# Reordering batch 1's q product and the last chunk of a fused attention and GLU kernel

## The chip, the cores and the metric

The kernel runs on one core of a Trainium2 chip. Its engines work beside each other and meet at semaphores: TensorE (PE in the profile, its weight loads PEld), VectorE (DVE), ScalarE (ACT), GpSimd (POOL) and SyncE (SP), which here only issues DMAs. The metric is the time of one execution on the device in microseconds. A run's time is a little longer than the span of its profile, which goes from the first instruction to the last.

## What is computed

```python
def phi(x):                                   # S1, S2: 8 x 32
    a = np.einsum('rd,bhsd->bhsr', S1, x)
    b = np.einsum('rd,bhsd->bhsr', S2, x)
    return np.einsum('bhsi,bhsj->bhsij', a, b).reshape(*x.shape[:-1], 64)
q_p, k_p = phi(q), phi(k)                     # q, k, v: batch 4, heads 4, sequence 1088, depth 32
kv = np.einsum('bhsf,bhsd->bhfd', k_p, v)
z = np.sum(k_p, axis=2)
num = np.einsum('bhsf,bhfd->bhsd', q_p, kv)
den = np.einsum('bhsf,bhf->bhs', q_p, z)[..., None] + 1e-06
x = (num / den).transpose(0, 2, 1, 3).reshape(4352, 128)
gate = 1.0 / (1.0 + np.exp(-(x @ w_gate)))    # w_gate, w_val: 128 x 1536
out = (gate * (x @ w_val)) @ w_out            # w_out: 1536 x 128
```

All data are fp32.

## The kernel before

**The second half sets the beat.** The 4352 tokens go in nine chunks: eight of 512 and a last one of 256. The 1536 hidden columns are 12 blocks of 128. A *wave* (`w1`, matmuls on L496) is one block of one chunk: gate and value products in one PSUM tile of two banks, from a pool of two such tiles. ACT takes the sigmoid of the gate half (`sg`, L504). DVE multiplies it with the value half (`g`, L537), which frees the tile for the wave after next. In the last chunk a wave covers two blocks of 256 tokens, so that it has six waves, and its gate is two DVE instructions (L530).

**The product with w_out follows some waves later.** A list `todo` holds each part with the wave number from which it may run. Chunk 0 uses plain products (`w2`, L379; two waves later). When the last of them is done, DVE transposes the result (L388) and SP issues four stores of 64 KB (L350). Chunks 1 to 7 take pairs of waves by a scheme with seven half products: `w2_a` (three waves after the odd wave) and `w2_b` (four), matmuls on L338. POOL makes the differences of tokens that they need (L328). At a chunk's end ACT copies part of the result and DVE adds (L435), spread over later waves by a list `late`. Chunk 8 uses `w2_end` (L400; three waves later, six parts of eight matmuls). Two half tiles of 128 tokens are collected in one PSUM tile of two banks, copied out by ACT (L409) and DVE (L410) into one SBUF tile, and stored by SP and ACT (L363). That SBUF tile and all earlier output tiles come from one tag, `o_sb`, with two buffers.

**`slot(group, waves)`** writes the order out by hand. It runs `group`, and then for each wave: the gate of the wave before (`glu`), one entry of `late` (two in the last chunk), all parts of `todo` that are due, and the next wave.

**The first half is fitted in between, batch by batch.** For batch 1 the steps are: transposes of k and q on DVE; `begin(1)`, which runs the gate, the k products (`kps`, L623) and the compact q products (`cqps`, L769), copies the latter to SBUF on ACT (L777), and then calls `spread`; the outer products for k (L702) and their sums (L876); the product of k with v (`kvz`, L842); two multiplies `qmult(1, 0)` and `qmult(1, 1)` on DVE (L822); and `parts(1)`, the numerators (L1207) and denominators (L971, L984).

**`spread`** turns the compact q products, 288 KB, into two operands of 1.1 MB: SP writes them to DRAM (`dq<-cq`, L787), waits until that has landed, and reads them back with repeats: `qp` and `bq` for the first q half, then for the second (L794), then eight small tables (L815). A `qmult` waits for the three reads of its half. The buffer of `bq` is the one that the next batch's k and q are loaded into.

PE, DVE, ACT and POOL run their instructions in the order of the program text. SP's DMAs are placed by the build, and each takes one of eight completion semaphores in turn, so that an issue can also wait for an older DMA on the same one.

Of the kernel before, what the change touches and what calls it, by code (L numbers as in the profile page):

```python
# [8 lines left out]
F32 = mybir.dt.float32  # L9
# [5 lines left out]
MUL = ALU.mult  # L15

P = 128
# [3 lines left out]
def kernel(  # L21
# [12 lines left out]
    nc = tc.nc  # L34

    B, H, S, D = q.shape
    R = S1.shape[0]
    F = R * R
    NTOK, DM = out.shape
    DFF = moe_w_gate.shape[1]  # L40
    NJ = DFF // P
    assert DM == H * D == P and D == 32 and R == 8 and S % 32 == 0 and NTOK % 512 == 256

    T = S // 32
# [4 lines left out]
    TCH = 512  # L49
# [292 lines left out]
    def store(ci, rows):  # L342
        t0, tw = tok_chk[ci]
        c = t0
        while c < t0 + tw:
            b, r = divmod(c, S)
            n = min(t0 + tw - c, S - r) // 32
            u = (c - t0) // 32
            for g4 in range(4):
                nc.sync.dma_start(  # L350
                    out=bass.AP(
                        tensor=out.tensor,
                        offset=out.offset + (b * S + r // 32) * DM + 32 * g4,
                        ap=[[T * DM, 32], [DM, n], [1, 32]],
                    ),
                    in_=rows(g4)[:, u : u + n, :],
                )
            c += n * 32

    def store_end(o_sb):  # L360
        b, r = divmod(tok_chk[-1][0], S)
        for c, eng in enumerate((nc.sync, nc.scalar)):
            eng.dma_start(  # L363
                out=bass.AP(
                    tensor=out.tensor,
                    offset=out.offset + (b * S + r // 32 + 16 * c * T) * DM,
                    ap=[[T * DM, 16], [1, 8 * DM]],
                ),
                in_=o_sb[64 * c : 64 * c + 64],
            )  # L370

    def w2(ci, j0, jn, g):
        if j0 == 0:
            moe["sum"] = ci
            moe["acc"] = pso.tile([P, TCH], F32, tag="acc0", name="moeout")
        for jj in range(jn):
            j = j0 + jj
            for d in (slice(0, P),) if j < NJ - 2 else (slice(0, 64), slice(64, P)):
                nc.tensor.matmul(  # L379
                    out=moe["acc"][d],  # L380
                    lhsT=w_sb[:, 2, j, d],
                    rhs=g[:, jj],
                    start=(j == 0),
                    stop=(j == NJ - 1),
                )
        if j0 + jn == NJ:
            o_sb = sbA.tile([P, 2, TCH // 32, 32], F32, tag="o_sb", name="o_sb")[:, 0]
            nc.vector.transpose(out=o_sb.rearrange("p t d -> p (t d)"), in_=moe["acc"])  # L388
            store(ci, lambda g4: o_sb[32 * g4 : 32 * g4 + 32])

    def w2_end(ci, j0, jn, g):
        if j0 == 0:
            moe["sum"] = ci
            moe["acc"] = ps2.tile([P, 2, TCH], F32, tag="two", name="moeout")
        acc = moe["acc"]
        for u in range(2):
            for jj in range(jn):
                j = j0 + jj
                for c in (u * P, u * P + 64):
                    nc.tensor.matmul(  # L400
                        out=acc[c % P : c % P + 64, u, :DM],
                        lhsT=g[:, jj, c : c + 64],
                        rhs=w_sb[:, 2, j, :],
                        start=(j == 0),
                        stop=(j == NJ - 1),
                    )
        if j0 + jn == NJ:
            o_sb = sbA.tile([P, 2, P], F32, tag="o_sb", name="o_end")
            nc.scalar.copy(out=o_sb[:, 0], in_=acc[:, 0, :DM])  # L409
            nc.vector.tensor_copy(out=o_sb[:, 1], in_=acc[:, 1, :DM])  # L410
            store_end(o_sb)


    fst = {}
# [66 lines left out]
    def w1():  # L481

        ci = moe["ci"]
        t0, tw = tok_chk[ci]
        jn = TCH // tw
        j0 = moe["w"] * jn
        wv = psm.tile([P, 2, TCH], F32, tag="wave", name="wave")

        tp = tw // 2 if ci == 0 and j0 == 0 else tw
        turn = (moe["w"] // 2) % 2  # L490
        for o in range(0, tw, tp):
            for which in range(2):
                for jj in range(jn):
                    for c in (0,) if ci == 0 else (1 - turn, turn):
                        d = slice(0, P) if ci == 0 else slice(64 * c, 64 * c + 64)
                        nc.tensor.matmul(  # L496
                            out=wv[d, which, jj * tw + o : jj * tw + o + tp],
                            lhsT=w_sb[:, which, j0 + jj, d],
                            rhs=xT[:, t0 + o : t0 + o + tp],
                            start=True,  # L500
                            stop=True,
                        )
        sg = sbG.tile([P, TCH], F32, tag="sg", name="sg")
        nc.scalar.activation(out=sg, in_=wv[:, 0], func=ACTF.Sigmoid)  # L504
        if ci == 0:
            if j0 == 1:
                narrow_01(2, 3)
            if 0 < j0 < NJ - 2:
                narrow_w(j0 + 1, 3)
            narrow_w(j0 + 2, 1)  # L510
            narrow_w(j0 + 2, 2)
            if j0 < 3:
                narrow_w(j0 + 3, 0)
            if j0 > 1:
                narrow_w(j0 + 4, 0)
            if j0 == NJ - 3:
                weight_sums(0, NJ // 4)
        if ci == 1 and j0 == 1:
            weight_sums(NJ // 4, NJ // 2)
        if moe["w"] % 2 == 0:  # L520
            moe["g"] = sbG.tile([P, 2, TCH], F32, tag="g", name="g")
        pair, odd, n = moe["g"], moe["w"] % 2, moe["n"]

        def glu():
            g = pair[:, odd]
            todo = moe["todo"]
            if jn == 2:
                for jj in range(2):
                    cols = slice(jj * tw, jj * tw + tw)
                    nc.vector.tensor_tensor(  # L530
                        out=g[:, cols].rearrange("p (u s y) -> p y u s", u=2, y=4),
                        in0=wv[:, 1, cols].rearrange("p (y u s) -> p y u s", u=2, y=4),
                        in1=sg[:, cols].rearrange("p (y u s) -> p y u s", u=2, y=4),
                        op=MUL,
                    )
            else:
                nc.vector.tensor_tensor(out=g, in0=wv[:, 1], in1=sg, op=MUL)  # L537
            if not fast(ci):
                lag = 3 if ci else 2
                part = (ci, j0, jn, g.rearrange("p (j t) -> p j t", j=jn))  # L540
                todo.append((n + lag, lambda: (w2_end if ci else w2)(*part)))
                return
            if not odd:
                moe["t"] = raw.tile([P, 4, HALF], F32, tag="w_in", name="tsum")
            token_sums(pair, moe["t"], odd)
            if odd:
                part = (ci, j0 // 2, pair, moe["t"])
                todo.append((n + 3, lambda: w2_a(*part)))
                todo.append((n + 4, lambda: w2_b(*part)))

        moe["gate"] = glu
        moe["w"] += 1
        moe["n"] += 1
        if j0 + jn == NJ:
            moe["ci"] += 1
            moe["w"] = 0
# [3 lines left out]
            moe["gate"]()  # L560
            moe["gate"] = None

    def slot(group, waves):

        if group is not None:
            group()
        todo = moe["todo"]
        for _ in range(waves):
            more = moe["ci"] < len(tok_chk)
            if more and sum(tok_chk[moe["ci"]]) > moe["ready"]:  # L570
                break
            glu()
            for _ in range(2 if moe["ci"] >= len(tok_chk) - 1 else 1):
                if moe["late"]:
                    moe["late"].pop(0)()
            while todo and todo[0][0] <= moe["n"]:
                todo.pop(0)[1]()
            if more:
                w1()
            elif not todo:  # L580
                break
            else:
                todo.pop(0)[1]()
# [236 lines left out]
    def qmult(b, n):  # L820
        q0 = half(QP[b], n)
        nc.vector.tensor_tensor(out=q0, in0=q0, in1=half(BQ[b], n), op=MUL)  # L822
# [358 lines left out]
    def begin(b):  # L1181
        glu()
        kps(b)
        cq[b] = qcomp(b, (0, 1), (psm, "wave"))
        spread(b, (0, 1), cq[b], nc.sync, nc.sync)
# [78 lines left out]
    slot(None, 1)  # L1264
    turn_q(1, 0)
    turn_q(1, 1)
    slot(lambda: begin(1), 1)
    for pi in range(2):
        outer(1, pi)
        slot(None, 1)  # L1270
# [7 lines left out]
    qmult(1, 0)  # L1278
    weights_z(1)
    slot(lambda: ndt(1), 1)  # L1280
    qmult(1, 1)
    load_kq(2)
    slot(None, 2)
    slot(lambda: parts(1), 1)

    def until(n):
# [63 lines left out]
```

## Time and profile before

| what | value |
|---|---|
| median of three runs | 296.4 us (295.51 to 296.53) |
| the profiled execution | 296.06 us |
| its span in the profile | 294.3 us |
| PE busy | 287.0 us, 98% of the span |
| chain that ended last: PE wave L496 | 51% |
| chain that ended last: PE prod L338 | 20% |
| chain that ended last: DMA qp<-dq | 4% |
| clock granted to PE | 1.00 |

In the profile a line reads: start, duration, engine, source line, operation, result and operands, count, and in brackets how long the engine stood idle before it and whose work ended that. In the chain of waits each piece is what the next one waited for, from the start to the last instruction. The ends of matmuls are modelled, so a short stall of PE can hide under the tail of the matmul before it; the distance from one wave's start to the next shows it better.

### The profile page before, as it was taken

The page shows a single profiled execution, that of the slowest core. Times are in us where ns is not written, and L with a number is a line of the kernel's source. Part 1 is how long each engine was busy: PE and PEld are TensorE (multiplying, and loading weights), DVE is VectorE, ACT ScalarE, POOL GpSimd, SP SyncE. Part 2 cuts the span into 40 slices and gives each one's busy share as a digit, 9 for nine tenths or more (in the row PEclk, how much of TensorE's full clock was granted, in tenths as well). Part 3 has the DMA queues.
Part 4 walks back from the last instruction along what each step waited for, and adds up shares of the span by engine and source line. Part 5 has one row for each costly group of instructions (what it writes and reads, how often), then busy time and mean ns, then how long its engine had stood idle before and what let it go on. Part 6 is the DMA issues. An engine that isn't in the chain of part 4 may idle for free.

```text
span 294.3 us, 5800 instructions
## 1 busy us (share of the span) xinstructions
PE 287.0 (98%) x2276; PEld 154.6 (53%) x2276; DVE 188.5 (64%) x326; ACT 92.1 (31%) x168; POOL 161.2 (55%) x221
## 2 busy tenths in 40 slices
PE   8899999999999999999999999999999999999994
PEld 3444433354455455554555555554555555555894
DVE  5998789977637766677556685668336433642463
ACT  3457542322223322322233213423232223322231
POOL 2365644894645657546446597664465655555200
PEclk9999999999999999999999999999999999999999
DMA  7993521584800167416000573102000200020002
GB/s 217 339 352 85 140 75 78 146 156 131 240 0 0 21 150 172 134 46 181 8 0 2 148 178 103 17 2 37 0 2 0 36 2 0 0 38 0 2 0 56
DMA packets 28762, 24.23 MB, mean 82 GB/s; under 512 B 18560, under 2 KB 23936, under 8 KB 28736
## 3 DMA queue, kind: packets, MB, share of 16 engines
q1 hardware_dynamic: 28288, 23.10, 30.2%
q10 hardware_dynamic: 448, 0.77, 0.9%
q8 instruction: 18, 0.29, 0.4%
q14 instruction: 8, 0.07, 0.1%
HBM read 20.60 MB, written 3.26 MB: 81 GB/s over the span
## 4 chain that ended last, share of the span: by engine, by line
PE 78%; DMA 7%; DVE 7%; POOL 2%; issue 2%; ACT 1%; SPq 1%; ACTq 0%; POOLq 0%
PE wave L496 51%; PE prod L338 20%; DMA qp<-dq 4%; POOL head L118 2%; PE moeout L400 2%; DVE head L109 2%; DMA kq<-in_k_dram 2%; DVE w_sb L127 2%; PE moeout L379 1%; DMA b<-dq 1%; DVE head L105 1%; PE nps L1207 1%; DVE qp L822 1%; PE kvz L842 1%; DMA dq<-cq 1%
## 5 line engine op out<-in xcount | busy, mean ns | idle before, releaser
L496 PE MATMUL wave<-xT,w_sb 128*64 128x512 f32 (+3 forms) x820 | 211.2, 566 | 0.6 <-DVE g L537 0.5
L496 PEld LDWEIGHTS wave<-xT,w_sb 128*64 128x64 f32 (+1 forms) x820 | 85.2, 140 | 64.4 <-issue 49.5
L504 ACT ACTIVATE sg<-wave 128x512 f32<-128x512 f32 x102 | 60.9, 597 | 173.8 <-PE wave L496 166.8
L537 DVE TENSOR_TENSOR g<-wave,sg 128x512 f32<-128x512 f32 x96 | 65.8, 686 | 75.3 <-ACT sg L504 74.1
L328 POOL TENSOR_TENSOR tsum<-g 128x256 f32<-128x256 f32 x84 | 67.8, 810 | 27.7 <-DVE g L537 27.5
L328 POOL TENSOR_TENSOR tsum<-g,tsum 128x256 f32<-128x256 f32 x42 | 34.2, 815 | 59.8 <-DVE g L537 59.6
L338 PE MATMUL prod<-tsum,ws 128*64 128x256 f32 x252 | 62.9, 381 | 0.0
L338 PEld LDWEIGHTS prod<-tsum,ws 128*64 128x64 f32 x252 | 31.3, 137 | 16.6 <-issue 12.3
L338 PE MATMUL prod<-g,w_sb 128*64 128x256 f32 x168 | 34.9, 383 | 0.0
L328 POOL TENSOR_TENSOR tsum<-tsum,g 128x256 f32<-128x256 f32 x42 | 32.7, 779 | 3.3
L338 PE MATMUL prod<-tsum,w_sb 128*64 128x256 f32 x84 | 25.4, 384 | 0.0
L338 PEld LDWEIGHTS prod<-g,w_sb 128*64 128x64 f32 x168 | 15.8, 137 | 18.2 <-issue 15.4
L338 PE MATMUL prod<-g,ws 128*64 128x256 f32 x84 | 25.0, 379 | 0.0
L118 POOL TENSOR_TENSOR head<-head,tail 128x384 int32<-128x384 int32 (+2 forms) x14 | 13.3, 953 | 18.2 <-DVE head L109 12.9
L338 PEld LDWEIGHTS prod<-g,ws 128*64 128x64 f32 x84 | 11.5, 137 | 3.8
L379 PE MATMUL moeout<-g,w_sb 128*128 128x512 f32 (+1 forms) x28 | 12.7, 611 | 0.3 <-DVE w_sb L127 0.3
L338 PEld LDWEIGHTS prod<-tsum,w_sb 128*64 128x64 f32 x84 | 10.9, 137 | 2.4 <-issue 1.9
L822 DVE TENSOR_TENSOR qp<-qp,bq 128x1152 f32<-128x1152 f32 (+1 forms) x7 | 9.6, 1376 | 3.4 <-DMA b<-dq 1.9
L702 DVE TENSOR_TENSOR kp<-kab 128x1152 f32<-128x1152 f32 (+2 forms) x10 | 10.8, 1094 | 0.0
L530 DVE TENSOR_TENSOR g<-wave,sg 128x256 f32<-128x256 f32 x12 | 6.6, 634 | 6.2 <-ACT sg L504 6.1
L470 DVE STREAM_TRANSPOSE o_sb<-res 64x512 f32<-64x512 f32 x14 | 9.5, 686 | 0.0
L435 DVE TENSOR_TENSOR res<-prod,other 64x512 f32<-64x512 f32 (+1 forms) x14 | 7.6, 541 | 2.6 <-ACT other L429 2.6
(121 smaller groups left out, 202.6 us busy)
## 6 DMA issues: line engine op xcount, KB each, us to landing
qp<-dq SPq DMA_DIRECT2D x7, 576.0 KB, 10.4
bq<-dq SPq DMA_DIRECT2D x14, 288.0 KB
kq<-in_k_dram SPq DMA_DIRECT2D x3, 544.0 KB, 4.0
kq<-in_q_dram SPq DMA_DIRECT2D x3, 544.0 KB
w_in<-in_moe_w_out_dram SPq DMA_DIRECT2D x6, 256.0 KB
w_in<-in_moe_w_gate_dram SPq DMA_DIRECT2D x5, 256.0 KB
w_in<-in_moe_w_val_dram SPq DMA_DIRECT2D x5, 256.0 KB, 6.9
out_dram<-o_sb SPq DMA_DIRECT2D x20, 64.0 KB, 1.9
```

Of the source, the lines that this page charges most:

```text
L118: nc.gpsimd.tensor_tensor(out=head, in0=head, in1=tail, op=ALU.add)
L328: nc.gpsimd.tensor_tensor(out=t[:, u], in0=in0, in1=in1, op=ALU.subtract)
L338: nc.tensor.matmul(out=out, lhsT=lhsT, rhs=rhs, start=start, stop=stop, skip_group_check=True)
L379: nc.tensor.matmul(out=moe["acc"][d], lhsT=w_sb[:, 2, j, d], rhs=g[:, jj], start=(j == 0), stop=(j == NJ - 1),)
L435: nc.vector.tensor_tensor(out=out, in0=in0, in1=in1, op=op)
L470: nc.vector.transpose(out=o_sb[:64, d].rearrange("p t x -> p (t x)"), in_=r[:, 1 + 2 * d : 3 + 2 * d].rearrange("p u x -> p (u x)"),)
L496: nc.tensor.matmul(out=wv[d, which, jj * tw + o : jj * tw + o + tp], lhsT=w_sb[:, which, j0 + jj, d], rhs=xT[:, t0 + o : t0 + o + tp], sta ...
L504: nc.scalar.activation(out=sg, in_=wv[:, 0], func=ACTF.Sigmoid)
L530: nc.vector.tensor_tensor(out=g[:, cols].rearrange("p (u s y) -> p y u s", u=2, y=4), in0=wv[:, 1, cols].rearrange("p (y u s) -> p y u s", ...
L537: nc.vector.tensor_tensor(out=g, in0=wv[:, 1], in1=sg, op=MUL)
L702: eng.tensor_tensor(out=KP[b][:, pi, j0:j1].rearrange("p j m (i l) -> p (j m) i l", i=R), in0=bass.AP(tensor=a0.tensor, offset=a0.offset, ...
L822: nc.vector.tensor_tensor(out=q0, in0=q0, in1=half(BQ[b], n), op=MUL)
```

## The change

Batch 1: `begin(1)` runs after the due w_out products of its slot instead of ahead of them, `qmult(1, 1)` and the load of batch 2's k and q come one slot later, and chunk 0's stores are put into `late`, to be issued with the next wave. In the built order of SP's queue, two of the four stores stand ahead of `dq<-cq` and two between it and the first `qp<-dq`; before, two stood between them and two after all of `spread`. The number of SP's DMAs is the same.

Last chunk: the gate is one DVE instruction per wave instead of two. The lag of `w2_end` is four waves instead of three. The last pair of chunk 7 (`early`) is multiplied one wave sooner. The two half tiles of the output lie in two PSUM tiles (tags `acc0` and `two`) and are copied into two SBUF tiles of tag `o_sb`, each stored by one engine as 128 runs of 512 B; before, each store had 64 runs of 1 KB.

```diff
-    def store_end(o_sb):
+    def store_end(acc):
         b, r = divmod(tok_chk[-1][0], S)
-        for c, eng in enumerate((nc.sync, nc.scalar)):
+        o_sb = [sbA.tile([P, P], F32, tag="o_sb", name="o_end") for _ in range(2)]
+        for u, copy in enumerate((nc.scalar.copy, nc.vector.tensor_copy)):
+            copy(out=o_sb[u], in_=acc[u])
+        for u, eng in enumerate((nc.scalar, nc.sync)):
             eng.dma_start(
                 out=bass.AP(
                     tensor=out.tensor,
-                    offset=out.offset + (b * S + r // 32 + 16 * c * T) * DM,
-                    ap=[[T * DM, 16], [1, 8 * DM]],
+                    offset=out.offset + (b * S + r // 32 + u) * DM,
+                    ap=[[T * DM, 32], [2 * DM, 4], [1, DM]],
                 ),
-                in_=o_sb[64 * c : 64 * c + 64],
+                in_=o_sb[u],
             )
...
-            store(ci, lambda g4: o_sb[32 * g4 : 32 * g4 + 32])
+            moe["late"].append(
+                lambda: store(ci, lambda g4: o_sb[32 * g4 : 32 * g4 + 32])
+            )
 
     def w2_end(ci, j0, jn, g):
         if j0 == 0:
             moe["sum"] = ci
-            moe["acc"] = ps2.tile([P, 2, TCH], F32, tag="two", name="moeout")
+            moe["acc"] = [
+                pso.tile([P, TCH], F32, tag="acc0", name="moeout0")[:, :DM],
+                ps2.tile([P, 2, TCH], F32, tag="two", name="moeout1")[:, 0, :DM],
+            ]
...
-                        out=acc[c % P : c % P + 64, u, :DM],
+                        out=acc[u][c % P : c % P + 64],
...
-            o_sb = sbA.tile([P, 2, P], F32, tag="o_sb", name="o_end")
-            nc.scalar.copy(out=o_sb[:, 0], in_=acc[:, 0, :DM])
-            nc.vector.tensor_copy(out=o_sb[:, 1], in_=acc[:, 1, :DM])
-            store_end(o_sb)
+            store_end(acc)
...
             if jn == 2:
-                for jj in range(2):
-                    cols = slice(jj * tw, jj * tw + tw)
-                    nc.vector.tensor_tensor(
-                        out=g[:, cols].rearrange("p (u s y) -> p y u s", u=2, y=4),
-                        in0=wv[:, 1, cols].rearrange("p (y u s) -> p y u s", u=2, y=4),
-                        in1=sg[:, cols].rearrange("p (y u s) -> p y u s", u=2, y=4),
-                        op=MUL,
-                    )
+                nc.vector.tensor_tensor(
+                    out=g.rearrange("p (j u s y) -> p j y u s", j=2, u=2, y=4),
+                    in0=wv[:, 1].rearrange("p (j y u s) -> p j y u s", j=2, u=2, y=4),
+                    in1=sg.rearrange("p (j y u s) -> p j y u s", j=2, u=2, y=4),
+                    op=MUL,
+                )
...
-                lag = 3 if ci else 2
+                lag = 4 if ci else 2
...
-                todo.append((n + 3, lambda: w2_a(*part)))
-                todo.append((n + 4, lambda: w2_b(*part)))
+                early = ci == len(tok_chk) - 2 and j0 == NJ - 1
+                todo.append((n + 3 - early, lambda: w2_a(*part)))
+                todo.append((n + 4 - early, lambda: w2_b(*part)))
...
-    def slot(group, waves):
+    def slot(group, waves, behind=None):
...
             while todo and todo[0][0] <= moe["n"]:
                 todo.pop(0)[1]()
+            if behind is not None:
+                behind()
+                behind = None
             if more:
                 w1()
...
-    slot(lambda: begin(1), 1)
+    slot(None, 1, behind=lambda: begin(1))
...
     slot(lambda: ndt(1), 1)
+    slot(None, 1)
     qmult(1, 1)
     load_kq(2)
-    slot(None, 2)
+    slot(None, 1)
     slot(lambda: parts(1), 1)
```

## The prediction

> **What bounds the kernel now.** I read the page first (shares, then the chain), then the chain in order of time, then the timelines of DVE, SP and the last 7 us, and the table of DMA issues.
>
> ```profile
> PE 287.0 (98%) x2276; PEld 154.6 (53%) x2276; DVE 188.5 (64%) x326; ACT 92.1 (31%) x168; POOL 161.2 (55%) x221
> ```
>
> TensorE (PE) is the bound, and almost without gaps: from 20 us to 290.4 us the window table shows 0.10 us idle in 40:60, 0.52 us in 60:80, and nothing else. No matmul is added or removed, so only three places can pay: the two stalls near 51 and 73 us, and what follows the last matmul. In order of time the chain of waits names the first two:
>
> ```profile
> 51.45 0.79 PE cqps L769 x16
> 52.26 0.65 ACT cq L777
> 52.93 2.08 DMA dq<-cq
> 56.94 10.88 DMA qp<-dq
> 67.84 4.01 DMA b<-dq
> 71.84 1.36 DVE qp L822
> 73.86 1.94 PE wave L496 x8
> ```
>
> Batch 1's q product is written to DRAM, read back spread, and multiplied on DVE. The second product (71.84) holds the gate of the wave that started at 67.95; the wave at 73.86 needs that gate's bank. DVE alone:
>
> ```profile
> 66.27 1.79 DVE L822 TENSOR_TENSOR qp<-qp,bq 128x1024 f32<-128x1024 f32 x1 [1.43 <-DMA bq<-dq]
> ...
> 69.23 0.68 DVE L537 TENSOR_TENSOR g<-wave,sg 128x512 f32<-128x512 f32 x1
> 71.84 1.36 DVE L822 TENSOR_TENSOR qp<-qp,bq 128x1152 f32<-128x1152 f32 x1 [1.93 <-DMA b<-dq]
> ```
>
> DVE idles twice for landings. The first wait costs PE nothing: the gate behind it ends at 69.91, and the wave that needs it starts at 70.54. The second does cost. SP's queue:
>
> ```profile
> 52.93 0.33 SPq L787 DMA_DIRECT2D dq<-cq  x1
> 53.97 0.87 SPq L350 DMA_DIRECT2D out_dram<-o_sb  x2
> 55.03 0.57 SPq L794 DMA_DIRECT2D qp<-dq  x1
> ```
>
> So the read-back starts when dq has landed, with two of chunk 0's stores issued in between; the other two come at 72.19. The end:
>
> ```profile
> 290.46 0.27 ACT L409 COPY o_end<-moeout 128x128 f32<-128x128 f32 x1 [2.11 <-PE moeout L400]
> 290.76 0.29 DVE L410 COPY o_end<-moeout 128x128 f32<-128x128 f32 x1 [1.27 <-ACT o_end L409]
> 291.08 0.62 ACTq L363 DMA_DIRECT2D out_dram<-o_end  x1
> 291.11 0.63 SPq L363 DMA_DIRECT2D out_dram<-o_end  x1
> ```
> ```profile
> out_dram<-o_sb SPq DMA_DIRECT2D x20, 64.0 KB, 1.9
> ...
> out_dram<-o_end SPq DMA_DIRECT2D x1, 64.0 KB, 2.3
> ```
>
> (The smallest stores, 16 KB, show 1.5 in the same column.) The two copies run one after the other, both stores start after the second, and they issue in 0.62 us side by side and land late (2.3 us).
>
> **What the Trainium skill says.** "Perfetto Trace Analysis", Per-instruction lifecycle (DMA Instruction, HWDGE): an issue locks the shared descriptor generator, and the recorded issue includes that lock wait. The trace agrees: two simultaneous issues took 0.62 and 0.63 us, a lone one (dq) 0.33. "DMA: Bandwidth & Descriptors", Queues, rings and completion order: on each DMA engine a queue's descriptors are taken up in ring order, so a store issued ahead on SP's queue is moved ahead. Before has no case of stores ahead of dq; I rest the delay below on it. The same page, Specifications: at least 512 B per transfer for full rate, below that slower. The new last stores have runs of exactly 512 B, the old ones 1 KB; no run here separates the two. "PSUM — Partial Sum Buffer", PSUM bank collisions: two engines must not use one bank and quadrant at once. The two halves of the old tile lie in different banks, so the 0.30 us between the copies is a dependency, not a bank.
>
> **The change part by part.** Times are on the clock of before.
>
> 1. *Chunk 0's last products ahead of batch 1's projections.* Removed: cqps starts at 51.45, 0.74 us after kps, though it takes 0.65 when nothing holds it (kps holds the same 16 records). Chunk 0's last product (0.91) then covers that wait, and the next wave's bank is free already (gate done at 52.15). New: product 50.61 to 51.5, kps 51.57, cqps 52.22, wave 52.87 instead of 53.01. Gain 0.14.
>
> 2. *The spread starts later.* cqps moves from 51.45 to 52.22; the copy ended 1.45 us after its start, so at 53.67; dq can be issued at 53.7. In the built order SP has two stores ahead of it. Their transpose (0.72) runs on DVE right after the gate, to 52.8; the stores issue 52.85 to 53.7 (0.87 for two). So SP is free just in time and dq is issued at 53.72, +0.79. The stores' data are partly ahead of dq's in the rings: 0 to 0.3 us more, I take 0.1. Stores three and four go out behind dq while it lands (2.08), so they cost the read-back nothing. All landings shift by s = 0.9; bounds 0.7 (nothing in the rings) and 1.5 (both stores' data fully ahead, and a lane wait).
>
> 3. *What s does.* The first multiply waits on a landing, so it and the gate behind it shift by s: gate ends at 69.91 + 0.9 = 70.81, wave at 70.86. PE would now be ready at 70.54 − 0.14 = 70.40. New stall 0.46, where there was none: gate slack 0.44 against s 0.9.
>
> 4. *The second multiply a slot later.* The gate that stood behind it now stands before it. The old stall: the wave at 70.54 takes 1.77 and the products after it 0.81, as in the pairs beside it, so 73.12 was possible and 73.86 came: 0.74 (0.52 shown; the rest is the modelled tail of the last matmul). It goes. The multiply now runs 72.74 to 74.1, the next gate to 74.8; the numerators want both at about 75.5. Covered by 0.7; beyond s = 1.6 it would cost. The next batch's k and q loads wait for this multiply, but were issued at 75.23 behind v's four, so they lose nothing.
>    Sum of 1 to 4: the wave at 73.86 moves to 70.86 + 2.58 = 73.44, gain 0.42. In general the gain is 1.32 − s, at most 0.88. PE is packed from there on, so it reaches the end.
>
> 5. *The last chunk.* Six gates, each two instructions taking 1.10, become one instruction each. Below: 0.69, as for a plain 512; above: 1.10. Nothing waits in either case, see 6.
>
> 6. *Lag four and one pair of products earlier.* On PE the same instructions in another order. Last sequence before: three parts after the last wave, 48 records in 2.79, at 0.87 per 16 a 2.61: stall 0.17 on the last gate. After, four parts (3.48) follow the last wave; sigmoid and gate need about 1.9, so the stall goes. New risks: the third and fourth waves stand back to back, the fourth needs the second's gate, with 0.6 us spare by my count; the sixth needs the fourth's gate, behind 2.03 us of chunk 7's sums on DVE: 0.4 spare. The early products need token differences that POOL finished at 273.88; they start at 274.66. Gain 0.17.
>
> 7. *Two PSUM tiles.* Tile 0's products end 0.43 before tile 1's, so ACT's copy is done before PE ends and its store leaves early. DVE copies straight after the last matmul: 0.30 gained. The DVE copy now waits for chunk 7's stores, because the second end tile takes their buffer. They leave two gates earlier (about 285.2 instead of 287.71); even if the last again lands 4.7 us after the first issue (the fourth was issued from 290.5 and takes 1.9) that is 289.9, before PE's end at 290.24. Covered, by 0.3.
>
> 8. *The last store's landing.* Old: 2.3 after issue, beside ACT's and right behind chunk 7's fourth store (issued until 291.01). New: alone, 64 KB in 128 runs. Bounds: 2.3 (nothing changes) and 1.5 (the smallest stores of the trace land so); I take 1.7. Gain 0.6.
>
> Sum: 0.42 + 0.17 + 0.30 + 0.60 = 1.5 at full value; I take off 0.1 for the doubled number of descriptors in the last stores, so 1.4. The profiled execution took 296.06 (span 294.3 and 1.76 around it): 294.7. Against the median of 296.4 it is 295.0. The three runs scatter over 1.0; I say 294.8.
>
> **The rivals.**
> A, the forecast: 294.8.
> B, the transfer takes the stall's place: s near 1.4, so the middle gives −0.1, and the last store still lands after 2.3: the end gives 0.47. 296.06 − 0.4 = 295.7. For it: each store's data are many small packets, and nothing in before shows dq behind them; against: dq is issued when most of them have gone.
> C, both stalls go: s at or under 0.44, the middle gives 0.88; the end gives 1.1: 294.1. For it: DVE waits 1.43 for the first landing, so any faster read-back is worth its full length; against: cqps alone starts 0.77 later.
> D, slower: dq is held by the stores, at SP's queue near 53 us, since the first store waits for DVE's transpose and everything behind it on SP waits too. Price 1:1 from s = 1.32; with 1.07 from the end it is slower from s = 2.4, and by over 0.5% from 3.9. At s = 4: 296.06 + 2.7 − 1.07 = 297.7. Against: the transpose needs only a product that ends at 51.7.
> That the built order doesn't do what it says is out: it shows all moves.
>
> **How the numbers follow.** A 0.48, B 0.30, C 0.16, D 0.06. Under 0.5% (1.5 us) a measurement of this kernel cannot be told from no change. A straddles that line: I give 0.29 of it to faster, 0.19 to same. With C, and 0.03 of B, faster is 0.48; same is 0.19 + 0.27 = 0.46; slower 0.06. The range goes from C's time less a little scatter, 293.9, to B's plus the same, 296.0.
>
> **What would show it.** Right: the read-back issued near 55.9; the first multiply near 67.2 and a wave held to about 70.9; no PE gap near 73; the DVE copy within 0.1 us of the last matmul; the last landing under 2 us. Wrong: a first multiply after 68, or an idle PE in the last chunk, or a DVE copy released by a store.

## The result and the profile after

The changed kernel takes 294.82 us (median of 6 runs, 294.29 to 295.32), the kernel before 296.46 (6 runs, 295.51 to 296.88): ratio 0.9947, interval 0.9926 to 0.9967. That is 1.64 us less, and the forecast of 294.8 was met. (A few executions took over 1.5% longer than their kernel's fastest; they are left out of the medians and ratios here.) Part of the agreement is luck: the last chunk's half of the sum came out close, but several steps inside both halves did not, and what the middle gives is known only roughly.

The profiled execution took 295.29 (span 293.5; before 296.06 and 294.3). TensorE's line on the page of the changed kernel:

```profile
PE 286.3 (98%) x2276; PEld 155.4 (53%) x2276; DVE 187.4 (64%) x320; ACT 92.1 (31%) x168; POOL 160.4 (55%) x221
```

The matmuls are the same in number and DVE has six instructions fewer, the joined gates. To see where the time went I cut each trace at matmuls that both kernels have: the first of chunk 0's fourth-last w_out product (near 42 us), the first product after batch 1's numerators (near 77), the last matmul's end, the end of the span. (The start is left out: the first wave begins 14.75 to 15.73 us into the span in all profiles but q_old_slot's, differing from run to run with the same code ahead of it. In this pair the first cut lies 0.57 us earlier after the change, by chance; with it the stretches add up to the 0.8 between the two spans.)

| stretch, us | before | after, profiled | what the forecast expected |
|---|---|---|---|
| middle, ~42 to ~77 | 34.96 | 35.52 (+0.56) | −0.42 |
| from there to the last matmul's end | 212.89 | 212.75 (−0.14) | −0.17 |
| last matmul to the span's end | 3.86 | 3.26 (−0.60) | −0.90 |

So the two gains behind the middle are there, and the middle lost time in this very execution. The chain of waits of the changed kernel, in order of time, beside the one shown of before:

```profile
53.71 2.32 DMA dq<-cq
...
59.18 14.70 DMA bq<-dq
73.89 1.74 DMA b<-dq
```

The write is issued at 53.71 instead of 52.93, and the read-back holds the path until 73.87, longer than before. The last small table (`b`, 36 KB) leaves only then, because its completion semaphore is the one that this last big read holds: in all 14 profiles it is issued 0.5 to 0.75 us after the read-back's last packet. What is held is no longer a wave. TensorE of the changed kernel, 71 to 79 us:

```profile
72.30 2.06 PE L501 MATMUL wave<-xT,w_sb 128*64 128x512 f32 x8
74.89 0.48 PE L978 MATMUL denj<-b,zw 64*32 64x160 f32 x8 [0.52 <-DMA b<-dq]
75.76 0.48 PE L978 MATMUL denj<-b,zw 64*32 64x160 f32 x8 [0.40 <-DMA b<-dq]
```

The wave that started at 73.86 after a stall now starts at 72.30 without one. The denominators after it multiply the last spread table (b) directly and wait for it twice. DVE of the changed kernel:

```profile
67.25 1.23 DVE L829 TENSOR_TENSOR qp<-qp,bq 128x1024 f32<-128x1024 f32 x1 [3.22 <-DMA a<-dq]
68.39 0.22 DVE L958 TENSOR_TENSOR zz<-kvd,unit 128x64 f32<-128x64 f32 x1
...
69.11 0.69 DVE L540 TENSOR_TENSOR g<-wave,sg 128x512 f32<-128x512 f32 x1
70.12 0.69 DVE L540 TENSOR_TENSOR g<-wave,sg 128x512 f32<-128x512 f32 x1 [0.33 <-ACT sg L509]
74.00 1.36 DVE L829 TENSOR_TENSOR qp<-qp,bq 128x1152 f32<-128x1152 f32 x1 [3.19 <-DMA a<-dq]
```

Compare the second multiply: 71.84 before, 74.00 now. Both gates stand ahead of it, as intended. The "a" named in the bracket is a neighbour on a shared semaphore: the multiply needs the big reads, and the last of these lands at 73.87, as the chain shows. Past the middle TensorE has no gap (200.00 busy), as the windows of the changed kernel show (window, us, then busy time of PE, PEld, DVE, ACT, POOL):

```profile
60.00:80.00 20.00, 19.08 (x232) 9.84 (x230) 11.90 (x21) 5.12 (x9) 12.56 (x21) 1.00 0.69 167
80.00:280.00 200.00, 200.00 (x1520) 111.81 (x1518) 116.41 (x182) 58.02 (x99) 115.15 (x148) 1.00 0.21 49
```

And the end, from the timeline of the changed kernel:

```profile
290.15 0.63 ACTq L366 DMA_DIRECT2D out_dram<-o_end  x1
290.29 0.29 DVE L364 COPY o_end<-moeout 128x128 f32<-128x128 f32 x1 [1.74 <-PE moeout L408]
290.61 0.64 SPq L366 DMA_DIRECT2D out_dram<-o_end  x1
```

DVE's copy is released by the matmuls (they end at 290.27), not by ACT's copy. The last store still issues in 0.64, though ACT's issue had run 0.46 us alone, and lands 2.0 us after its issue (290.61 to 292.60).

### The profile page after: what moved, and what is told of

The parts are those of the page before. It is cut to its first block, busy times and chain, and to the rows that moved or that the text cites. A ratio compares the mean times of both kernels' runs of the same rounds, so it can differ in the third digit from the quotient of the medians.

```text
span 293.5 us, 5784 instructions
## 1 busy us (share of the span) xinstructions
PE 286.3 (98%) x2276; PEld 155.4 (53%) x2276; DVE 187.4 (64%) x320; ACT 92.1 (31%) x168; POOL 160.4 (55%) x221
## 2 busy tenths in 40 slices
DMA packets 28890, 24.23 MB, mean 83 GB/s; under 512 B 18560, under 2 KB 24064, under 8 KB 28864
## 3 DMA queue, kind: packets, MB, share of 16 engines
HBM read 20.60 MB, written 3.26 MB: 81 GB/s over the span
## 4 chain that ended last, share of the span: by engine, by line
PE 76%; DMA 15%; SPq 3%; DVE 3%; POOL 1%; issue 1%; ACT 0%; POOLq 0%
PE wave L501 49%; PE prod L338 20%; DMA bq<-dq 7%; DMA v<-in_v_dram 3%; DMA w_in<-in_moe_w_out_dram 2%; PE moeout L408 2%; POOL head L118 1%; DMA kq<-in_k_dram 1%; PE moeout L382 1%; SPq L801 1%; PE nps L1214 1%; SPq L157 1%; DMA dq<-cq 1%; PE kvz L849 1%; DVE w_sb L127 1%
## 5 line engine op out<-in xcount | busy, mean ns | idle before, releaser
L540 DVE TENSOR_TENSOR g<-wave,sg 128x512 f32<-128x512 f32 x96 | 65.9, 686 | 75.7 <-ACT sg L509 74.5
L328 POOL TENSOR_TENSOR tsum<-g 128x256 f32<-128x256 f32 x84 | 66.9, 798 | 31.6 <-DVE g L540 31.4
L338 PEld LDWEIGHTS prod<-g,w_sb 128*64 128x64 f32 x168 | 15.7, 137 | 18.2 <-issue 15.4
L533 DVE TENSOR_TENSOR g<-wave,sg 128x512 f32<-128x512 f32 x6 | 6.5, 1087 | 4.7 <-ACT sg L509 4.7
```

The lines of the kernel that those rows point to most:

```text
L328: nc.gpsimd.tensor_tensor(out=t[:, u], in0=in0, in1=in1, op=ALU.subtract)
L338: nc.tensor.matmul(out=out, lhsT=lhsT, rhs=rhs, start=start, stop=stop, skip_group_check=True)
L533: nc.vector.tensor_tensor(out=g.rearrange("p (j u s y) -> p j y u s", j=2, u=2, y=4), in0=wv[:, 1].rearrange("p (j y u s) -> p j y u s", j ...
```

## The experiments

Two questions were left by this result: why a kernel whose middle grew in the profile was faster by the full forecast, and which parts carry the gain. In the first expectations P is the theory that the read-back's landing decides the middle and differs between executions; Q, that the middle gives the predicted 0.4 and the first profile caught a slow read-back. Times are medians, each against the kernel before in the same of three series of runs (296.31, 296.16 and 296.27).

**The change again.** after_again is the changed kernel unaltered.

> The changed kernel once more, unaltered, to see how far its profile repeats. Theory P (the read-back's landing decides the middle, and it differs from execution to execution): ratio 0.993 to 0.997; PE again stalls before the denominators (L978) on a table of the read-back, by anything between 0 and 1 us, and the distance from the first dq issue to the last table's issue again lies between 19 and 21 us. Theory Q (the middle gives the predicted 0.4 us and the first profile caught a slow read-back): same ratio, no stall over 0.2 us before the denominators.

Measured: 294.59, ratio 0.9952 (0.9935 to 0.9969), as in the first result. But its profile has another middle, 33.96 instead of 35.52, and from dq to the last table it is 18.5 us, outside the expected 19 to 21. TensorE of this second execution of the same program:

```profile
73.08 1.94 PE L501 MATMUL wave<-xT,w_sb 128*64 128x512 f32 x8
74.95 0.50 PE L978 MATMUL denj<-b,zw 64*32 64x160 f32 x16
```

No wait. The 4.6 KB packets of batch 1's read-back took 14.2 us here, 15.9 in the first profile. So 33.96 is the middle with nothing late, the floor of this order, and the first profile lay 1.56 above it (0.92 as shown gaps, the rest in the modelled ends of the matmuls before them). That is what P says: the landing decides, and it differs between executions of one program. Two profiles alone don't show it; more follow below.

**Each half alone.** mid_only has the edits of batch 1 (projections behind the products, the q slot, the store put off) and the old last chunk; end_only the reverse.

```diff
 # mid_only (part: the gate, the early pair and the stores go back too)
-                lag = 4 if ci else 2
+                lag = 3 if ci else 2
-            moe["acc"] = [
...
+            moe["acc"] = ps2.tile([P, 2, TCH], F32, tag="two", name="moeout")
 # end_only (part: the stores' place in `late` goes back too)
-    slot(None, 1, behind=lambda: begin(1))
+    slot(lambda: begin(1), 1)
...
-    slot(None, 1)
     qmult(1, 1)
     load_kq(2)
-    slot(None, 1)
+    slot(None, 2)
```

> Only the changes around batch 1 (projections behind w_out's products, second q multiply and chunk 0's stores a slot on); the last chunk as before. Theory P: no gain, 296.1 to 296.7 us where before takes 296.4: the stall before the wave goes and one before the denominators comes. Theory Q: 0.4 us faster, 295.7 to 296.1.

> Only the changes in the last chunk; batch 1 as before. Both theories: from the last matmul's end to the end of the span 3.1 to 3.4 us where before shows 3.9, and PE's last stall of 0.17 gone: 0.7 to 0.9 us in all, 295.4 to 295.8 us where before takes 296.4. Theory P adds that this is about half of what the whole change gave in its timed runs or more (over 0.7 of 1.64); if it gives 1.4 or more, the middle gives nothing at all.

Measured: mid_only 295.86, ratio 0.9987 (0.9964 to 1.0009), not told apart from no change; end_only 295.34, ratio 0.9962 (0.9947 to 0.9977). The end is worth 0.97 us (296.31 − 295.34). What batch 1's edits add is known less well: by medians 0.45 from mid_only and 0.75 from 295.34 − 294.59, by the ratios 0.4 and 0.3. mid_only's time lies in Q's range, yet its profile shows P's stall at the table (0.38 before the denominators) with a middle of 34.97, that of before; behind its last matmul lie 3.99 us (3.86 before). end_only, with batch 1 as before, has before's stall of the wave again (0.40) and a middle of 34.83.

**The stores out of dq's way.** In sp_text SP keeps the order of the program text, which puts dq and the whole read-back ahead of chunk 0's four stores.

```diff
                 mybir.EngineType.Pool,
+                mybir.EngineType.SP,
             }
```

> The changed kernel with SP's DMAs in the order of the program text too, so that dq goes out as soon as its copy is done and chunk 0's four stores stand behind the whole read-back. Theory P: first qp read issued 0.8 to 1.1 us sooner against cqps' start than in the changed kernel (4.5 us there, 3.5 here), no stall over 0.2 us before the denominators, 0.3 to 0.9 us faster than the changed kernel: 293.9 to 294.5 us. Theory Q: the stores ahead cost nothing in the end, 294.5 to 295.1, as the changed kernel.

SP's timeline of sp_text:

```profile
53.01 0.35 SPq L795 DMA_DIRECT2D dq<-cq  x1
55.12 0.57 SPq L802 DMA_DIRECT2D qp<-dq  x1
...
71.56 2.00 SPq L351 DMA_DIRECT2D out_dram<-o_sb  x4
```

and that of the changed kernel:

```profile
52.24 1.42 SPq L350 DMA_DIRECT2D out_dram<-o_sb  x2
53.71 0.49 SPq L794 DMA_DIRECT2D dq<-cq  x1
54.25 1.03 SPq L350 DMA_DIRECT2D out_dram<-o_sb  x2
56.05 0.58 SPq L801 DMA_DIRECT2D qp<-dq  x1
...
73.89 0.31 SPq L822 DMA_DIRECT2D b<-dq  x1
```

The edit does what it says: the read-back's first issue comes 3.57 us after the start of cqps, in the changed kernel 4.53 to 4.71. The middle was 33.97, the floor. Yet the time is 294.50, ratio 0.9936 (0.9911 to 0.9961), which overlaps the unaltered kernel's. A repeat was run for the interval:

> The kernel of sp_text once more, unaltered, to narrow its time. Theory P: again no stall of PE between 45 us and the last wave, 294.0 to 294.6 us and a ratio to before under 0.995. Theory Q: 294.5 to 295.1.

Measured: 294.69, ratio 0.9939 (0.9916 to 0.9963). Its read-back took 15.5 us and cost 0.23 before the numerators, a middle of 34.56; P had expected no stall. So the stores' order moves the start of the transfer by about 1 us, but the transfer's own length varies by more, and the order alone isn't measurable in the time.

**Which of the two moves in the middle pays.** q_old_slot undoes the later q product, begin_old undoes the later projections.

```diff
 # q_old_slot
     slot(lambda: ndt(1), 1)
-    slot(None, 1)
     qmult(1, 1)
     load_kq(2)
-    slot(None, 1)
+    slot(None, 2)
 # begin_old
-    slot(None, 1, behind=lambda: begin(1))
+    slot(lambda: begin(1), 1)
```

> The changed kernel with the second q multiply and the k and q loads back in their old slot. Theory P (the read-back lands about 1 us later in the changed kernel, and only the moved multiply keeps it off PE): the stall before the wave is back and longer than before's, PE idle 1.2 to 2.2 us there (0.52 in before), 295.3 to 296.2 us where the changed kernel takes 294.7. Theory Q (the projections' new place is what pays): 294.6 to 295.0.

> The changed kernel with batch 1's projections back ahead of w_out's products; multiply, stores and last chunk as changed. In the build dq then stands ahead of chunk 0's stores. Theory P: the read-back starts 0.9 to 1.1 us sooner against cqps, so no stall over 0.2 us before the denominators, and the 0.14 us before cqps return: 294.2 to 294.8 us, not slower than the changed kernel. Theory Q: slower than the changed kernel by 0.1 to 0.3 us.

q_old_slot: 297.48, ratio 1.0044 (1.0017 to 1.0071), 1.3 us above the kernel before where the changed kernel lies 1.5 to 1.7 below it, and slower than either theory expected. Its profile shows the old stall again (TensorE's granted clock was 0.983 in it, so only the order of events is read). DVE, then TensorE:

```profile
76.20 1.36 DVE L829 TENSOR_TENSOR qp<-qp,bq 128x1152 f32<-128x1152 f32 x1 [3.33 <-DMA a<-dq]
```
```profile
78.22 3.04 PE L501 MATMUL wave<-xT,w_sb 128*64 128x512 f32 x8 [2.37 <-DVE g L540]
```

In the middle, moving the projections without the multiply thus costs: the spread starts later, and the multiply that still stands ahead of a gate hands the delay to a wave.

begin_old: 294.08, ratio 0.9929 (0.9911 to 0.9947), lower than the changed kernel in the other series. SP's timeline of begin_old:

```profile
52.41 0.33 SPq L794 DMA_DIRECT2D dq<-cq  x1
53.45 0.87 SPq L350 DMA_DIRECT2D out_dram<-o_sb  x2
54.51 0.58 SPq L801 DMA_DIRECT2D qp<-dq  x1
...
70.08 0.31 SPq L822 DMA_DIRECT2D b<-dq  x1
```

and its window over batch 1's spread, where the changed kernel's had 19.08:

```profile
60.00:80.00 20.00, 20.00 (x241) 10.05 (x239) 13.98 (x23) 5.72 (x10) 14.42 (x21) 1.00 0.66 179
```

dq goes out ahead of every store, the last table is issued at 70.08, and TensorE has no gap. Its middle is 34.22: 0.25 above the changed kernel's floor, but met without a stall. It was repeated beside the changed kernel, and with SP in text order as well:

> The changed kernel a third time, beside the next two on the same chip. 294.4 to 295.0 us. Theory P: between the first matmul of chunk 0's second last w_out product (near 42 us) and the first product after batch 1's numerators, 33.9 to 35.6 us, whatever is over 34.0 being a stall before the denominators that ends with a table's landing.

> The kernel of begin_old again. Theory P (the read-back has about 1 us more room there than in the changed kernel, at the price of 0.25 us before and around cqps): the same distance 34.2 to 34.4 us with no stall before the denominators, 294.0 to 294.5 us, faster than the changed kernel by 0.2 to 0.8 us. Rival: its first time was luck of the chip, and it equals the changed kernel within 0.2 us.

> begin_old with SP's DMAs in the order of the program text, so that no store of chunk 0 stands near the read-back. Theory P: the two stores between dq and the first read cost nothing there (they hide in dq's landing), so the first read is issued 3.6 us after cqps' start in both, and the time is begin_old's within 0.3 us: 293.9 to 294.5 us. Rival: the stores still slow the read-back, and it is 0.3 us or more faster than begin_old.

Measured: after_third 294.74, ratio 0.9947 (0.9929 to 0.9964); begin_old_2 294.06, ratio 0.9926 (0.9907 to 0.9946); begin_old_text 294.25, ratio 0.9930 (0.9910 to 0.9950). The intervals overlap, but begin_old is 0.7 lower beside the changed kernel and came out alike in both series, and its middle is 34.22 in all three profiles, though the read-back took 13.5 us in one and 15.4 in another. The changed kernel's is 35.52, 33.96 and 35.36, with 15.9, 14.2 and 15.6; their mean, 34.95, lies 0.73 above 34.22. Text order adds nothing to begin_old, since there dq is ahead already. begin_old is the version that beats both kernels.

Together the profiles show that the landing decides. In those with the projections behind the products and the multiply moved, the middle follows the time from the first cut to the end of the read-back's last 4.6 KB packet:

| run | last packet ends, us after the cut | middle, us |
|---|---|---|
| sp_text | 28.48 | 33.97 |
| end_flat | 29.50 | 33.97 |
| after_again | 29.74 | 33.96 |
| sp_text_2 | 29.97 | 34.56 |
| end_lag3 | 30.48 | 34.84 |
| mid_only | 30.72 | 34.97 |
| after_third | 31.15 | 35.36 |
| after | 31.37 | 35.52 |

In begin_old's three it ends at 27.30, 29.62 and 29.24, before anything waits for it.

**The last stores' pattern.** end_flat is sp_text with the two last stores written as one stretch of memory each, over rows of batch 0; it leaves out the last 256 tokens.

```diff
-                    offset=out.offset + (b * S + r // 32 + u) * DM,
-                    ap=[[T * DM, 32], [2 * DM, 4], [1, DM]],
+                    offset=out.offset + u * P * DM,
+                    ap=[[DM, P], [1, DM]],
```

> The kernel of sp_text, except that the two last stores write their 128 runs of 512 B one behind another, over rows of batch 0 (the last 256 tokens of the output are left out), instead of spread over batch 3's rows. Theory E1 (the spread pattern makes the last issues long): they take 0.3 to 0.45 us instead of 0.64, and the last landing comes 1.7 us after its issue instead of 2.0. Theory E2 (an issue at the end is long whatever its pattern): 0.6 us and 2.0 us as before.

Measured: 293.29 in one run. Timeline of end_flat:

```profile
288.60 0.36 ACTq L367 DMA_DIRECT2D out_dram<-o_end  x1
...
289.06 0.35 SPq L367 DMA_DIRECT2D out_dram<-o_end  x1
```

Same tiles, same bytes, same copies: the issue takes 0.35 instead of 0.64, the landing 1.54 us instead of 2.0, and the stretch behind the last matmul 2.81 instead of 3.26. The packets are the same too: the page of each counts 28890, 24064 of them under 2 KB, and the last stores' are of 512 B in both. So it is the pattern of addresses, and not packet size, that costs (the flat form also lies in other rows). A stride alone isn't enough, since chunk 7's stores, each 512 runs of 128 B, issue in 0.32 to 0.50.

**Two tiles without lag and early products.**

```diff
-                lag = 4 if ci else 2
+                lag = 3 if ci else 2
...
-                early = ci == len(tok_chk) - 2 and j0 == NJ - 1
+                early = False
```

> The changed kernel with the lag of three waves in the last chunk and the last pair of chunk 7 in its old place; one gate instruction, two PSUM tiles and the new stores kept. By the prediction PE's last stall of 0.1 to 0.2 us is back (48 records of the last products in 2.7 to 2.8 us where 2.61 are needed), and from PE's end to the end of the span it is 3.25 us as in the changed kernel, so that the two PSUM tiles and the stores alone carry the 0.6 us there. Rival: the tail is longer, since DVE's last copy then waits for chunk 7's stores, which leave a gate later.

Measured: 299.54 in one run, 4.7 us over the changed kernel; the stretch ahead of the last matmul's end is 2.26 longer than the changed kernel's, the one behind it 2.25. From the timeline of its last 9 us, then TensorE earlier, then the chain of waits of the end:

```profile
289.24 3.03 SPq L350 DMA_DIRECT2D out_dram<-o_sb  x4
...
294.45 0.29 DVE L364 COPY o_end<-moeout 128x128 f32<-128x128 f32 x1 [3.44 <-DMA out_dram<-o_end]
```
```profile
281.19 1.09 PE L408 MATMUL moeout<-w_sb,g 128*64 128x128 f32 x16 [1.72 <-DVE res L440]
```
```profile
292.06 1.98 DMA out_dram<-o_end
294.04 0.03 issue
294.06 0.05 DVEq L364
```

Both buffers that the two tiles borrow are taken too early. The first last-chunk product waits 1.72 for a PSUM bank that chunk 7's sum on DVE still reads. DVE's copy waits 3.44. It needs the buffer of chunk 7's stores, which leave from 289.24, the last of them landing at 293.76, 4.5 us later. In the built program it also waits for ACT's store of the other tile, which lands at 294.04, and then DVE works through its list of semaphores until 294.45. Lag and early products aren't a small extra; together they pay for the two tiles (the run undoes both, so their shares are open).

## Why the prediction was right, step by step

Step 1 (projections behind products, 0.14): 0.25. The floor of the middle is 33.97 with the projections moved and 34.22 without. Mis-sized, in the safe direction.

Step 2 (spread later, s = 0.9): wrong in size. I had dq at +0.79, with SP free just in time. On before's clock (the cut near 42 us as the common point) dq came 1.35 us later in the first profile and 1.43 in the second. The term that failed is 0.87 for two stores: they took 1.42, of which the second 1.03 (0.48 before). And s isn't one number: the first multiply came 1.55, 1.22 and 1.26 later in the three profiles, the issue of the last table 2.62, 1.0 and 2.46. The forecast treated the read-back as a fixed length that shifts; it takes 13.5 to 15.9 us.

Step 3 (new stall of 0.46 at the wave): not there, in any of the three. I moved multiply and gate by s and kept their durations. They took less: from the first multiply's start to the gate's end 3.64 before, 2.55 after, because the multiply went from 1.79 to 1.23 and the small product behind it from 0.74 to 0.22. POOL before:

```profile
66.94 1.71 POOL L328 TENSOR_TENSOR tsum<-g 128x256 f32<-128x256 f32 x1
```

and after:

```profile
66.42 0.73 POOL L328 TENSOR_TENSOR tsum<-g 128x256 f32<-128x256 f32 x1
```

Before, token differences ran beside DVE's multiply, and the multiply and this difference are long (1.71 instead of 0.73). After, POOL had finished at 67.15, just before the multiply at 67.25. In the other two profiles of the changed kernel the multiply took 1.29 and the small product 0.21. The Trainium skill says why such pairs hold each other up: "SBUF — State Buffer", Who interferes with whom: a DVE instruction with two SBUF inputs contends with a GpSimd instruction that reads SBUF. The traces agree: in all 14 profiles the small product takes 0.74 or 0.75 where a token difference overlaps it and 0.21 or 0.22 where none does. No run here moves only that.

Step 4 (second multiply a slot later): the mechanism holds. The old stall of 0.74 is gone in all three profiles, and 34.96 − 34.22 = 0.74 in begin_old, where nothing else in the middle changed but chunk 0's stores. q_old_slot shows the other side. What the step left out is what is late next: it named the numerators as the next to want the landing, with 0.7 spare. The denominators come before them and read the last table themselves, without a multiply between, and that table is issued only when the last big read has landed. That cost 1.56 in the first profile, 1.39 in the third and nothing in the second.

So the middle's 0.42 came from errors that work against each other: no stall at the wave, more from the projections, a new stall at the tables in some executions. Timed, it is 0.3 to 0.75, which holds the forecast but doesn't confirm it; the mean middle of the three profiles, 34.95, is as long as before's one, 34.96. The changed kernel's ten times in the third series fall into five from 294.13 to 294.50 and five from 294.97 to 295.55 (the profiled one, with the stall, is 295.55). That fits a stall that comes and goes, but the 21 of the first series show no such split.

Step 5 (joined gate, 0.69 to 1.10): 1.05 to 1.10, the upper bound. Nothing waited, as said.

Step 6 (0.17): holds. The last 64 records take 3.51 without a gap, and the stretch before the end is 0.14 shorter.

Step 7 (0.30): holds. DVE's copy starts 0.02 us after the last matmul. The guard that I put at 0.3 was 1.75: chunk 7's stores landed at 288.54. end_lag3 shows that the danger named there is real.

Step 8 (0.6 for the landing): half of it. The stretch behind the last matmul lost 0.60; step 7 is 0.30 of that, so 0.3 is left. The store landed after 2.0, not 1.7. The reason was wrong: I took the slow issue for two stores sharing a lock, but it stays 0.64 with the other nearly done. end_flat, with 0.35, shows that it is the pattern of the store.

The end was put at 1.07 less 0.1. The profile gives 0.14 + 0.60 = 0.74, the timed runs of end_only 0.97. Against the rivals: B (a transfer takes the stall's place, −0.1 in the middle) is what the first profile shows there, with −0.56, and C (both stalls go, 0.88) the second, with 1.00; A, between them, is the median. D needed s of 2.4 to be slower; s reached 2.6 at the last table, and as I read it the time held because the new waiter stands later than the old.

Open: why the read-back's length differs between executions; why the second of the two stores ahead of dq is slow to issue; and 0.4 to 0.5 us of begin_old's gain, which is 2.1 to 2.2 timed, while 0.74 in the middle and 0.97 at the end make 1.7.

For the slow issue the traces have a suspect. In the 14 profiles 55 DMA issues took over 0.95 us, and every one overlaps a 16 KB packet of the instruction queue (q8) and ends 0.22 to 0.44 us after it. The reverse doesn't hold: in before, dq's issue of 0.33 overlaps such a packet. No run moves one, so the cause isn't shown.

For begin_old's surplus: before's stall ends with a landing too, so it should vary as well, and its 0.74 is from one execution that was faster than the median (296.06 against 296.46). The times fit, 294.63 to 298.53 over before's 77 runs and 293.81 to 294.76 over begin_old's 12, but before was profiled only once.

## What to carry to other kernels

When a multiply that waits for a transfer is moved behind a gate, list everything that reads that transfer, not only the multiply: the earliest of the others is the next to stall. And look at when the last small transfer can be issued: here a 36 KB table waited for a big read's semaphore (no run sends the tables first). Where a transfer's length varied between executions, slack was worth more than a shorter floor: begin_old gives up 0.25 us of TensorE's time, starts the read-back 1.2 to 1.8 us earlier after the first cut and is 0.7 us faster. Before borrowing a buffer to cut a dependency, check when its last reader, a store above all, lets go.

## What the runs showed of the hardware

A read-back of the same bytes in the same program took 14.2, 15.6 and 15.9 us in three executions.

Two stores of 64 KB issue in 0.35 and land in 1.54 us as flat stretches, and need 0.64 and 2.0 us as 128 strided runs of 512 B.

Four stores of 64 KB issued from 289.24 in end_lag3 had landed 4.5 us later, those from 285.12 in the changed kernel 3.4 us later.

All 55 DMA issues over 0.95 us overlap a 16 KB packet of the instruction queue and end 0.22 to 0.44 us after it.

DVE's 128x1024 multiply took 1.79 us beside POOL's differences and 1.23 when POOL was idle; the 128x64 product 0.74 and 0.22. Not both sides need be long: in begin_old_2 the multiply took 1.23 beside a difference of 1.82.
